# A row scale applied later, and VectorE's steps put into one fixed sequence, in a fused attention and SoLU kernel

## The chip, the core and the metric

The kernel runs on one core of one Trainium2 chip. A core has five engines that work side by side, each with a queue of its own that it goes through in order: TensorE (PE in the profile, its weight loads PEld), VectorE (DVE), ScalarE (ACT), GpSimd (POOL) and SyncE (SP, which issues transfers here). An instruction at the head of a queue waits for the semaphores of the work that it needs, and everything behind it on that engine waits too. The metric is the device time of one execution in microseconds (us), lower is better.

## What is computed

Two stages, 33280 tokens (8 x 4160) of width 192, all in float32.

```
# stage 1, 8 heads of 24 columns, 7 taps: a causal sliding sum with softmax weights
w   = softmax(weight_gen, axis=-1)             # (8, 4160, 8, 7); sum + 1e-9 below
x   = sum over k of w[..., k] * x_padded[s + k]
# stage 2
h    = x @ w_in                                # 192 -> 1024
e    = exp(h - max(h)); sm = e / (sum(e) + 1e-9)
solu = h * sm
ln   = (solu - mean) / sqrt(var + 1e-6) * g_ln # mean and var over the 1024
out  = ln @ w_out                              # 1024 -> 192
```

## The kernel before

The tokens are laid over 128 partitions as 128 runs of 260 tokens, and a **tile** t is the t-th token of every run: 260 tiles, each a 128 x 192 block of x and a 128 x 1024 block of h. Stage 1 works on groups of four tiles, its weights and x come in chunks of sixteen.

The steps have short names, and a table `ops` maps each to a function. For one group or chunk of stage 1:

- `t0` to `t6` (`softmax_taps`, lines 104 to 130): softmax of a chunk's weights, on DVE, POOL, ACT, DVE, ACT, DVE, POOL.
- `att` (`attention`, lines 132 to 152): three large GpSimd instructions for four tiles, the 7-tap product `pr` and two foldings that leave two or three partial sums in `half` (two buffers).
- `fin` (line 396): VectorE reduces `half` to `a` (three buffers of four tiles). `dup` (line 402): ScalarE copies columns.

For one tile, or a pair, of stage 2:

- `xT`, `xhi`, `xn`, `xlo` or `xld` (lines 407 to 448): transposes on PE, split of x into a high and a low part.
- `mm1` (line 459): ten matmuls of 512 columns into `h`, which has three PSUM buffers, so that `mm1` of tile t+3 waits for the last readers of tile t.
- `max` (line 473, DVE): minus the row maximum. `vb` (line 477, DVE): a bound, the larger of that maximum's size and 0.5. `vr` (line 482, DVE): its reciprocal, the row scale SIGMA.
- `exp` (line 486, ACT): the exponentials `e` and their sum. `solu` (line 492, DVE): h becomes h x SIGMA x e, in place, with the row sum. The profile shows the read of that sum as an instruction of its own, DVE_READ_ACCUMULATOR.
- `sq` (line 498, ACT): squares for the variance. `hi` (line 505, ACT): h x 2^14 rounded to float16. `lo` (line 509, DVE): the rest in float16. `sq` and `lo` read the same PSUM tile, and whichever comes later in the program waits for the other.
- `tr` (line 517, SP): a transposing transfer of both halves. `mm2` (line 561): 24 matmuls into `po`. `out` (line 572, ACT): the row's factor, and every four tiles a store.
- `f0` to `f7` (`scales`, lines 521 to 552): per group of four tiles, eight tiny instructions on [128, 4] statistics, alternately ACT and DVE, that make the row's factor.

**What sets the order.** The steps are not written in the order in which they run. `plan` (lines 651 to 793) lists every step with its engine, a duration and the steps that it follows, `issue_order` (lines 806 to 866) plays them against a model of the engines, and where several are ready takes the one with the lowest tile number plus a number of the table `URGENCY`. The order that comes out is the order of the engines' queues. On the chip nothing of the model is left but that order.

Of the kernel before, what the change touches and what calls it, by code (L numbers as in the profile page):

```python
# [9 lines left out]
F32 = mybir.dt.float32  # L10
# [10 lines left out]
MIDDLE, REACH = 1.01538, 0.061529  # L21

# [7 lines left out]
def tile_kernel(ctx: ExitStack, tc: tile.TileContext, x, weight_gen, w_in, w_out, g_ln, out):  # L30
    nc = tc.nc
# [277 lines left out]
    def prepare_second(step, half=None):  # L309
# [11 lines left out]
        elif step == 6:  # L321
# [9 lines left out]
            nc.vector.tensor_scalar_add(kinv, k, (127 - 73 + 1) << 23)  # L331
# [133 lines left out]
    ZE, SIGMA, Q, E, Y, V, Y2, R, OUT, M, Z, U, L, T, NMAX, HALF, BOUND = range(17)  # L465
    stats = const.tile([P, 6, TG, 17], F32, name="stats")
# [23 lines left out]
    def solu(t):  # L490
        h, e = h_of[t], e_of[t]
        nc.vector.scalar_tensor_tensor(  # L492
            out=h, in0=h, scalar=stat(t, SIGMA), in1=e, op0=ALU.mult, op1=ALU.mult, accum_out=stat(t, M)
        )
# [8 lines left out]
    def high_half(t):  # L503
        hl = hl_of[t] = big.tile([P, 2, FF], F16, name="hl", bufs=3)
        nc.scalar.activation(hl[:, 0, :], h_of[t], AF.Copy, scale=2.0**14)  # L505

    def low_half(t):
        hl = hl_of[t]
        nc.vector.scalar_tensor_tensor(  # L509
            out=hl[:, 1, :], in0=h_of[t], scalar=2.0**14, in1=hl[:, 0, :],  # L510
            op0=ALU.mult, op1=ALU.subtract,
        )
# [8 lines left out]
    def scales(t, step):  # L521
# [86 lines left out]
    for n in range(8):  # L608
        ops[f"f{n}"] = at(scales, n)
# [38 lines left out]
}  # L648


def plan(run, starts, group, stat_group, rows_left, on_vector, loads):
# [74 lines left out]
    for i, t in enumerate(groups):  # L726
# [13 lines left out]
    for t in range(0, run, 2):  # L740
        add("xT", t, PE, 355, 300, ("dup", group_of[t]), low_of(t - 2))
# [158 lines left out]
```

## Time and profile before

| | |
|---|---|
| median of three runs | 1310.42 us (1307.23 to 1311.84) |
| the profiled execution | 1309.91 us, of which the span from first to last instruction is 1308.1 |
| busy share of the span | PE 95%, DVE 95%, POOL 91%, ACT 88% |
| granted TensorE clock | 0.994 of full speed |
| `max`, `lo`, `solu` on DVE, 260 each | 1218, 1222 and 1283 ns |
| `exp`, `sq`, `hi` on ACT, 260 each | 1124, 1130 and 1027 ns |
| `vb`, `vr` on DVE, 260 each | 154 and 161 ns |

How to read it: a duration is that of one instruction from start to end, and two that follow each other on DVE or ACT overlap a little, so the distance from start to start is what an instruction costs its queue. Four engines are busy for nine tenths of the span, and no single line of the page says which of them holds the others up.

### The profile page before, as it was taken

The numbers are of one execution on the slowest core, as the hardware profiler recorded it, in microseconds if no ns is written. First come the engines' busy times: TensorE is split into PE (matmuls) and PEld (weight loads), VectorE is DVE, ScalarE is ACT, GpSimd is POOL, SyncE is SP. The second block draws the span as 40 slices with busy tenths as digits, with TensorE's granted clock in tenths as the row PEclk, the third lists the DMA queues.
The fourth block names the chain that finished last, engine by engine and source line by source line (L and its number), as shares of the span: only waits on it lengthen the run. The fifth ranks groups of instructions, "written<-read, shape, count | busy, mean of one in ns | idle before, by whom it ended". The sixth has DMA issues, their size and how long they took to land.

```text
span 1308.1 us, 25825 instructions
## 1 busy us (share of the span) xinstructions
PE 1239.4 (95%) x9574; PEld 1069.3 (82%) x9574; DVE 1247.9 (95%) x2055; ACT 1151.4 (88%) x2271; POOL 1195.8 (91%) x243
## 2 busy tenths in 40 slices
PE   1689999999999999999999999999999999999998
PEld 1577788788888888888888888888888888888887
DVE  6889999999999999999999999999999999999995
ACT  5778888899899989989898989989898998998896
POOL 6999989999999999999999999999999999999910
PEclk9899999999999999999999999999999999999999
DMA  8488658697787969777796987788797876975665
GB/s 236 87 184 181 144 130 175 136 203 140 165 174 144 212 127 204 140 174 167 151 205 132 199 143 167 170 162 189 137 203 141 176 165 141 199 140 119 132 139 130
DMA packets 565917, 211.35 MB, mean 162 GB/s; under 512 B 544552, under 2 KB 545960, under 8 KB 565792
## 3 DMA queue, kind: packets, MB, share of 16 engines
q1 hardware_dynamic: 565344, 208.14, 76.3%
q10 hardware_dynamic: 448, 1.57, 0.5%
q8 instruction: 75, 1.23, 0.4%
q14 instruction: 50, 0.41, 0.1%
HBM read 46.15 MB, written 25.56 MB: 55 GB/s over the span
## 4 chain that ended last, share of the span: by engine, by line
DVE 51%; ACT 24%; issue 16%; PE 7%; DMA 2%; ACTq 0%; SPq 0%; DVEq 0%
DVE h L492 19%; DVE stats L473 15%; ACT e L486 9%; DVE a L396 8%; ACT e L498 5%; ACT hl L505 5%; PE h L459 3%; PE po L561 3%; ACT x_hi L421 2%; DVE hl L509 2%; ACT ot L572 2%; DVE stats L477 2%; DVE wm L114 1%; DVE wm L122 1%; DVE stats L529 1%
## 5 line engine op out<-in xcount | busy, mean ns | idle before, releaser
L135 POOL TENSOR_TENSOR pr<-xt,wt 128x5376 f32<-128x5376 f32 (+1 forms) x66 | 631.4, 9567 | 10.2 <-DMA wt<-in_weight_gen_dram 7.5
L561 PE MATMUL po<-w_hl,hlT 128*128 128x192 f16 x6192 | 557.4, 247 | 13.6 <-ACT ot L572 11.7
L561 PEld LDWEIGHTS <-hlT 128*128 128x128 f16 x6240 | 513.9, 98 | 61.6 <-issue 55.4
L492 DVE SCALAR_TENSOR_TENSOR h<-h,stats,e 128x1024 f32<-128x1024 f32 x260 | 333.5, 1283 | 4.5 <-ACT e L486 4.4
L509 DVE SCALAR_TENSOR_TENSOR hl<-h,hl 128x1024 f16<-128x1024 f32 x260 | 317.7, 1222 | 6.6 <-ACT e L498 2.9
L473 DVE TENSOR_REDUCE stats<-h 128x1 f32<-128x1024 f32 x260 | 316.8, 1218 | 3.7 <-PE h L459 3.0
L486 ACT ACTIVATE e<-h,stats 128x1024 f32<-128x1024 f32 x260 | 292.2, 1124 | 19.1 <-DVE stats L473 10.4
L498 ACT ACTIVATE e<-h,stats 128x1024 f32<-128x1024 f32 x260 | 293.7, 1130 | 7.0 <-DVE hl L509 5.7
L505 ACT ACTIVATE hl<-h 128x1024 f16<-128x1024 f32 x260 | 266.7, 1027 | 25.3 <-DVE h L492 23.4
L459 PE MATMUL h<-wb,x_lo 128*128 128x512 f32 x784 | 216.2, 397 | 0.0
L459 PE MATMUL h<-wa_hi,x_hi 128*128 128x512 f32 x520 | 180.3, 428 | 18.1 <-ACT e L498 10.7
L459 PEld LDWEIGHTS h<-wb,x_lo 128*128 128x128 f32 x784 | 148.6, 190 | 35.7
L147 POOL TENSOR_TENSOR pr<-pr 128x2304 f32<-128x2304 f32 (+1 forms) x34 | 169.6, 4987 | 2.7
L142 POOL TENSOR_TENSOR half<-pr 128x2304 f32<-128x2304 f32 x32 | 164.1, 5128 | 2.5
L459 PE MATMUL h<-wa_hi,x_lo 128*128 128x512 f32 x520 | 164.9, 398 | 1.4 <-ACT x_lo L435 1.4
L459 PE MATMUL h<-wa_lo,x_hi 128*128 128x512 f32 x520 | 164.0, 396 | 0.8 <-DVE wa_lo L268 0.8
L396 DVE TENSOR_REDUCE a<-half 128x768 f32<-128x2304 f32 (+1 forms) x66 | 149.1, 2259 | 0.4
L572 ACT ACTIVATE ot<-po,stats 128x192 f32<-128x192 f32 x258 | 110.7, 429 | 9.5 <-PE po L561 7.6
L459 PEld LDWEIGHTS h<-wa_hi,x_lo 128*128 128x128 f32 x520 | 98.3, 189 | 24.9 <-ACT x_lo L435 1.8
L459 PEld LDWEIGHTS h<-wa_lo,x_hi 128*128 128x128 f32 x520 | 98.3, 189 | 23.7 <-DVE wa_lo L268 1.6
L149 POOL TENSOR_TENSOR half<-pr 128x1536 f32<-128x1536 f32 (+1 forms) x34 | 114.8, 3377 | 2.7
L413 PE MATMUL pa<-ident,a 128*128 128x128 f32 x520 | 80.4, 276 | 27.6 <-DVE a L396 25.2
(77 smaller groups left out, 1132.7 us busy)
## 6 DMA issues: line engine op xcount, KB each, us to landing
out_dram<-ot SPq DMA_DIRECT2D x65, 384.0 KB, 3.4
xt<-in_x_dram SPq DMA_DIRECT2D x30, 576.0 KB, 4.7
xt<-in_x_dram SPq DMA_DIRECT2D x30, 480.0 KB, 4.5
wt<-in_weight_gen_dram SPq DMA_DIRECT2D x15, 448.0 KB, 4.5
hlT<-hl SPq DMA_TRANSPOSE x260, 4.3
hlT<-in_moe_w_out_dram SPq DMA_DIRECT2D x4, 384.0 KB, 5.4
xt<-in_x_dram SPq DMA_DIRECT2D x3, 384.0 KB, 5.1
hlT<-in_moe_w_in_dram ACTq DMA_DIRECT2D x2, 512.0 KB, 9.2
```

What stands on the lines that cost most here:

```text
L135: nc.gpsimd.tensor_tensor(out=window(pr, 0, [(TG * D, K), (HG, n * H), (1, HG)]), in0=window(xt, t * D, [(D, K), (HG, n * H), (1, HG)]), i ...
L142: nc.gpsimd.tensor_tensor(out=half, in0=pr[:, :3], in1=pr[:, 3:6], op=ALU.add)
L147: nc.gpsimd.tensor_tensor(out=pr[:, :3], in0=pr[:, :3], in1=pr[:, 3:6], op=ALU.add)
L396: nc.vector.tensor_reduce(columns(t)[:, :, :D], half.rearrange("p j t d -> p t d j"), axis=AX.X, op=ALU.add)
L459: nc.tensor.matmul(h[:, fs], lhs, rhs[:, fs], start=n == 0, stop=n == len(terms) - 1)
L473: nc.vector.tensor_reduce(stat(t, NMAX), h_of[t], axis=AX.X, op=ALU.max, negate=True)
L486: nc.scalar.activation(e, h_of[t], AF.Exp, bias=stat(t, NMAX), accum_out=stat(t, Z))
L492: nc.vector.scalar_tensor_tensor(out=h, in0=h, scalar=stat(t, SIGMA), in1=e, op0=ALU.mult, op1=ALU.mult, accum_out=stat(t, M))
L498: nc.scalar.activation(e_of.pop(t), h_of[t], AF.Square, bias=stat(t, M), scale=-float(FF), accum_out=stat(t, Q),)
L505: nc.scalar.activation(hl[:, 0, :], h_of[t], AF.Copy, scale=2.0**14)
L509: nc.vector.scalar_tensor_tensor(out=hl[:, 1, :], in0=h_of[t], scalar=2.0**14, in1=hl[:, 0, :], op0=ALU.mult, op1=ALU.subtract,)
L561: nc.tensor.matmul(po[:, :D], hlT[:, half * NJ + j, :], w2_hl[:, j, w, :], start=n == 0, stop=n == len(terms) - 1,)
```

## The change

SIGMA no longer enters `solu`. There the factor is the constant `BOOST` = 2^10, and SIGMA becomes the scale operand of `hi` and of `lo`, one value per partition read from memory where a constant stood before. The statistics that follow are then those of the unscaled row, so that `f0` and `f1` (which multiplied the sum of exponentials by the bound) fall away, 67 of each in the run, `f2` takes the sum directly with a small bias tile `least`, and `f7` multiplies three values in place of two. The places in `stats` are renumbered for that.

In `plan`, a function `turn` ties VectorE's steps of a tile, from tile 4 on, to one sequence: `max` of t+1 behind `vr` of t, `lo` of t behind `max` of t+1, `vb` of t+1 behind `lo` of t, `solu` of t+1 behind `vb`, `vr` behind `solu`. `hi` now follows `vr`. Some of the model's durations change by a few ns, `fin` of three sums from 2480 to 2705 ns. `URGENCY` is unchanged. The order of all queues is worked out anew from this.

```diff
+BOOST = 2.0**10
...
-            nc.vector.tensor_scalar_add(kinv, k, (127 - 73 + 1) << 23)
+            nc.vector.tensor_scalar_add(kinv, k, (127 - 73 + 15) << 23)
...
+    EPSILON = 1e-3 * FF**1.5 * BOOST
+    least = const.tile([P, 1], F32, name="least")
+    nc.gpsimd.memset(least, EPSILON * 1e-9)
...
     def solu(t):
-            out=h, in0=h, scalar=stat(t, SIGMA), in1=e, op0=ALU.mult, op1=ALU.mult, accum_out=stat(t, M)
+            out=h, in0=h, scalar=BOOST, in1=e, op0=ALU.mult, op1=ALU.mult, accum_out=stat(t, M)
...
     def high_half(t):
-        nc.scalar.activation(hl[:, 0, :], h_of[t], AF.Copy, scale=2.0**14)
+        nc.scalar.activation(hl[:, 0, :], h_of[t], AF.Copy, scale=stat(t, SIGMA))
     def low_half(t):
-            out=hl[:, 1, :], in0=h_of[t], scalar=2.0**14, in1=hl[:, 0, :],
+            out=hl[:, 1, :], in0=h_of[t], scalar=stat(t, SIGMA), in1=hl[:, 0, :],
...
-        if step == 0:
-            nc.scalar.activation(of(ZE), of(Z), AF.Copy, bias=1e-9)
-        elif step == 1:
-            reduce(U, ZE, 2, ALU.mult)
-        elif step == 2:
-            nc.scalar.activation(of(E), of(U), AF.Square, scale=1e-3 * FF**1.5)
+        if step == 2:
+            nc.scalar.activation(of(E), of(Z), AF.Square, bias=least, scale=EPSILON)
...
-            reduce(OUT, Y2, 2, ALU.mult)
+            reduce(OUT, Y2, 3, ALU.mult)
...
+FIXED = 4
+    def turn(name, t):
+        return [(name, t, -9999)] if FIXED <= t < run else []
...
-        add("max", t, DVE, 1131, 84, ("mm1", t), ("exp", t - 4))
-        add("vb", t, DVE, 62, 84, ("max", t), ("f7", ...))
-        add("vr", t, DVE, 70, 93, ("vb", t))
+        add("max", t, DVE, 1131, 84, ("mm1", t), ("exp", t - 4), *turn("vr", t - 1))
+        add("vb", t, DVE, 62, 84, ("max", t), ("f7", ...), *turn("lo", t - 1))
+        add("vr", t, DVE, 80, 83, ("vb", t), *turn("solu", t))
-        add("solu", t, DVE, 1200, 89, ("exp", t), ("vr", t))
+        add("solu", t, DVE, 1200, 89, ("exp", t), *turn("vb", t))
-        add("hi", t, ACT, 904, 120, ("solu", t), ("tr", t - 3))
-        add("lo", t, DVE, 1131, 90, ("hi", t))
+        add("hi", t, ACT, 904, 120, ("solu", t), ("vr", t), ("tr", t - 3))
+        add("lo", t, DVE, 1131, 90, ("hi", t), *turn("max", t + 1))
```

Three places of the queues show what moved. In the rows the lines are those of each kernel's own text, where the changed one has `max` at 478, `vb` 482, `vr` 487, `exp` 491, `solu` 497, `sq` 503, `hi` 510, `lo` 514, `fin` 398; a number behind a name tells one buffer from another.

**VectorE, tile 132 of 260.** Before, from one `max` to the next:

```order
L473 TENSOR_REDUCE stats_137<-h_8115 128x1
L477 TENSOR_REDUCE stats_137<-stats_137 128x1
L529 TENSOR_REDUCE stats_137<-stats_137 128x4
L482 RECIPROCAL stats_137<-stats_137 128x1
L509 SCALAR_TENSOR_TENSOR hl_8168<-h_8049,hl_8168 128x1024
L492 SCALAR_TENSOR_TENSOR h_8115,stats_137<-h_8115,stats_137,e_8186 128x1024
L529 TENSOR_REDUCE stats_137<-stats_137 128x4
```

And the same tile now:

```order
L478 TENSOR_REDUCE stats_137<-h_8097 128x1
L534 TENSOR_REDUCE stats_137<-stats_137 128x4
L514 SCALAR_TENSOR_TENSOR hl_8145<-h_8009,stats_137,hl_8145 128x1024
L482 TENSOR_REDUCE stats_137<-stats_137 128x1
L497 SCALAR_TENSOR_TENSOR h_8097,stats_137<-h_8097,e_8159 128x1024
L534 TENSOR_REDUCE stats_137<-stats_137 128x4
L487 RECIPROCAL stats_137<-stats_137 128x1
```

`max`, `lo` of the tile before, `solu` stood in this sequence already; `vb` has moved behind `lo` and `vr` behind `solu`, so that neither follows directly on the instruction whose result it reads.

**ScalarE, tiles 206 to 208.** Before, between one `exp` and the next one:

```order
L486 ACTIVATE e_12638,stats_137<-h_12565,stats_137 128x1024
L572 ACTIVATE ot_12643<-po_12590,stats_137 128x192
L498 ACTIVATE e_12579,stats_137<-h_12500,stats_137 128x1024
L421 CAST x_hi_12675<-pa_12622 128x512
L505 ACTIVATE hl_12677<-h_12565 128x1024
L486 ACTIVATE e_12682,stats_137<-h_12627,stats_137 128x1024
```

And now, over two tiles:

```order
L491 ACTIVATE e_12622,stats_137<-h_12514,stats_137 128x1024
L573 ACTIVATE ot_12542<-po_12594,stats_137 128x192
L437 CAST x_lo_12644<-pa_12537 128x512
L510 ACTIVATE hl_12653<-h_12514,stats_137 128x1024
L503 ACTIVATE e_12622,stats_137<-h_12514,stats_137 128x1024
L491 ACTIVATE e_12686,stats_137<-h_12579,stats_137 128x1024
L537 ACTIVATE stats_137<-stats_137,least_138 128x4
L573 ACTIVATE ot_12542<-po_12661,stats_137 128x192
L510 ACTIVATE hl_12709<-h_12579,stats_137 128x1024
L503 ACTIVATE e_12686,stats_137<-h_12579,stats_137 128x1024
L423 CAST x_hi_12738<-pa_12656 128x512
L491 ACTIVATE e_12742,stats_137<-h_12633,stats_137 128x1024
```

Before, the `exp` of the next tile stood directly behind `hi`, and the `sq` of the tile before it ahead of `hi`. Now `sq` of the same tile, and in the second case a cast of x as well, stands between `hi` and the next `exp`.

**VectorE, where the last groups are reduced.** Before, the 51st of the 66 reductions `fin` (it makes tiles 196 to 199) and what stands around it:

```order
L473 TENSOR_REDUCE stats_137<-h_11665 128x1
L477 TENSOR_REDUCE stats_137<-stats_137 128x1
L482 RECIPROCAL stats_137<-stats_137 128x1
L509 SCALAR_TENSOR_TENSOR hl_11715<-h_11603,hl_11715 128x1024
L396 TENSOR_REDUCE a_11738<-half_11496 128x4x192
L529 TENSOR_REDUCE stats_137<-stats_137 128x4
```

And now:

```order
L514 SCALAR_TENSOR_TENSOR hl_11072<-h_10936,stats_137,hl_11072 128x1024
L482 TENSOR_REDUCE stats_137<-stats_137 128x1
L497 SCALAR_TENSOR_TENSOR h_10994,stats_137<-h_10994,e_11106 128x1024
L487 RECIPROCAL stats_137<-stats_137 128x1
L398 TENSOR_REDUCE a_11124<-half_10871 128x4x192
L478 TENSOR_REDUCE stats_137<-h_11047 128x1
```

Counted along the queue, 192 `max` stood ahead of this `fin` before (tiles 0 to 191), and 182 stand ahead of it now: the `max` in the last row is that of tile 182. Ahead of the last `fin` it was 251 and is 242. In tiles, `fin` ran four to six ahead of `max` from tile 40 on before; now the distance starts at five and grows to fifteen by tile 192, where it stays.

More of the change, by code (lines that the diff above doesn't have):

```diff
@@ L462, in first_product @@
         h_of[t] = h
-    ZE, SIGMA, Q, E, Y, V, Y2, R, OUT, M, Z, U, L, T, NMAX, HALF, BOUND = range(17)
-    stats = const.tile([P, 6, TG, 17], F32, name="stats")
+    Q, E, Y, V, Y2, R, BOUND, OUT, M, Z, L, T, NMAX, HALF, SIGMA = range(15)
+    stats = const.tile([P, 6, TG, 15], F32, name="stats")
+    EPSILON = 1e-3 * FF**1.5 * BOOST
+    least = const.tile([P, 1], F32, name="least")
+    nc.gpsimd.memset(least, EPSILON * 1e-9)
     nc.gpsimd.memset(stats[:, :, :, HALF], 0.5)
@@ L607, in tile_kernel @@
         ops[f"lx{n}"] = at_chunk(load_x, n)
-    for n in range(8):
+    for n in range(2, 8):
         ops[f"f{n}"] = at(scales, n)
@@ L731, in plan @@
             after += [(f"lx{k}", starts[c]) for k in range(loads)]
-        add("att", t, POOL, part * (16850 if three else 18480), 60, *after, ready=12000 if c == 1 else 7500)
+        add("att", t, POOL, part * (16850 if three else 18480), 60, *after, ready=14200)
         old = t // 4 * 4 - 12
-        add("fin", t, DVE, part * (2480 if three else 1697), 92, ("att", t), ("xT", old + 2 if old >= 0 else -1))
+        add("fin", t, DVE, part * (2705 if three else 1697), 92, ("att", t), ("xT", old + 2 if old >= 0 else -1))
         add("dup", t, ACT, 295 if group(t) == 4 else 200, 112, ("fin", t))
@@ L740, in plan @@
     for t in range(0, run, 2):
-        add("xT", t, PE, 355, 300, ("dup", group_of[t]), low_of(t - 2))
+        add("xT", t, PE, 362, 300, ("dup", group_of[t]), low_of(t - 2))
         add("xhi", t, ACT, 465, 115, ("xT", t), ("mm1", t - 3))
@@ L755, in plan @@
             after.append(("mm1", t - 1, -9999))
-        add("mm1", t, PE, 2328, 72, *after)
-        add("max", t, DVE, 1131, 84, ("mm1", t), ("exp", t - 4))
-        add("vb", t, DVE, 62, 84, ("max", t), ("f7", stats_of[t - 24] if t >= 24 else -1, -9999))
-        add("vr", t, DVE, 70, 93, ("vb", t))
+        add("mm1", t, PE, 2332, 72, *after)
+        add("max", t, DVE, 1131, 84, ("mm1", t), ("exp", t - 4), *turn("vr", t - 1))
+        add("vb", t, DVE, 62, 84, ("max", t), ("f7", stats_of[t - 24] if t >= 24 else -1, -9999), *turn("lo", t - 1))
+        add("vr", t, DVE, 80, 83, ("vb", t), *turn("solu", t))
         add("exp", t, ACT, 1089, 31, ("max", t), ("sq", t - 2, -9999))
-        add("solu", t, DVE, 1200, 89, ("exp", t), ("vr", t))
+        add("solu", t, DVE, 1200, 89, ("exp", t), *turn("vb", t))
         add("sq", t, ACT, 1089, 32, ("solu", t))
-        add("hi", t, ACT, 904, 120, ("solu", t), ("tr", t - 3))
-        add("lo", t, DVE, 1131, 90, ("hi", t))
+        add("hi", t, ACT, 904, 120, ("solu", t), ("vr", t), ("tr", t - 3))
+        add("lo", t, DVE, 1131, 90, ("hi", t), *turn("max", t + 1))
         add("tr", t, SP, 60, 0, ("lo", t), ("mm2", t - 6), dma=-2600)
@@ L767, in plan @@
         after += [("mm1", run - 1), ("out", t - 2)] if t >= run - 4 else [("out", t - 1)]
-        add("mm2", t, PE, 1923, 218, ("tr", t), *after)
+        add("mm2", t, PE, 1930, 218, ("tr", t), *after)
         add("out", t, ACT, 303, 125, ("mm2", t), ("f7", stats_of[t]), ("od", t // 4 * 4 - 5))
@@ L771, in plan @@
             tiles = range(t - n + 1, t + 1)
-            add("f0", t, ACT, 97, 116, *(("exp", u, -160) for u in tiles))
-            add("f1", t, DVE, 70, 87, ("f0", t), *(("vr", u) for u in tiles))
-            add("f2", t, ACT, 97, 116, ("f1", t))
+            add("f2", t, ACT, 97, 116, *(("exp", u, -160) for u in tiles))
             add("f3", t, DVE, 70, 87, ("f2", t), *(("sq", u) for u in tiles))
```

## The prediction

> **What bounds it now.** I read the page first, then a long steady stretch, then the queues of VectorE and ScalarE row by row, since the page alone leaves four engines equal.
>
> ```profile
> span 1308.1 us, 25825 instructions
> ...
> PE 1239.4 (95%) x9574; PEld 1069.3 (82%) x9574; DVE 1247.9 (95%) x2055; ACT 1151.4 (88%) x2271; POOL 1195.8 (91%) x243
> ...
> DVE 51%; ACT 24%; issue 16%; PE 7%; DMA 2%; ACTq 0%; SPq 0%; DVEq 0%
> ```
>
> The chain of waits runs over VectorE and ScalarE. The columns of the next two rows are the stretch, its length, and the busy time of PE, PEld, DVE, ACT and POOL; the two below them are pieces of the chain, the start of every second three-sum `fin`, eight tiles apart.
>
> ```profile
> 50.00:250.00 200.00, 179.64 (x1341) 154.85 (x1342) 184.98 (x297) 163.37 (x322) 191.34 (x42) 0.97 0.73 155
> 300.00:1150.00 850.00, 845.06 (x6600) 731.27 (x6599) 839.35 (x1383) 775.98 (x1524) 821.87 (x157) 1.00 0.81 166
> ```
> ```profile
> 288.52 2.80 DVE a L396
> ...
> 1122.13 2.81 DVE a L396
> ```
>
> Between them lie 22 steps of eight tiles: 833.6 / 176 = 4.74 us a tile. PE is busy 99.4% of the second stretch, VectorE 98.7%, GpSimd 96.7%, ScalarE 91.3%. So nothing can go much below 4.71 us a tile whatever VectorE saves: PE's own work is 0.994 x 4.74. That is the first thing against a large gain. VectorE's queue over one plain tile, `solu` to `solu`:
>
> ```profile
> 632.96 1.28 DVE L492 SCALAR_TENSOR_TENSOR h<-h,stats,e 128x1024 f32<-128x1024 f32 x1
> 634.15 0.14 DVE L492 DVE_READ_ACCUMULATOR h<-h,stats,e 128x1 f32 x1
> 634.15 1.22 DVE L473 TENSOR_REDUCE stats<-h 128x1 f32<-128x1024 f32 x1
> 635.41 0.15 DVE L477 TENSOR_REDUCE stats<-stats 128x1 f32<-128x2 f32 x1
> 635.60 0.16 DVE L482 RECIPROCAL stats<-stats 128x1 f32<-128x1 f32 x1
> 635.68 1.22 DVE L509 SCALAR_TENSOR_TENSOR hl<-h,hl 128x1024 f16<-128x1024 f32 x1
> 636.82 1.28 DVE L492 SCALAR_TENSOR_TENSOR h<-h,stats,e 128x1024 f32<-128x1024 f32 x1
> ...
> 638.02 1.22 DVE L473 TENSOR_REDUCE stats<-h 128x1 f32<-128x1024 f32 x1
> ```
>
> Start to start, 634.15 to 638.02: `max` 1.26, `vb` 0.19, `vr` 0.08, `lo` 1.14, `solu` 1.20, together 3.87 us.
>
> **The VectorE part.** `vb` reads what `max` writes, and `vr` what `vb` writes. Where an independent reduction follows `max`, it starts sooner:
>
> ```profile
> 656.40 1.21 DVE L473 TENSOR_REDUCE stats<-h 128x1 f32<-128x1024 f32 x1
> 657.53 1.07 DVE L114 TENSOR_REDUCE wm<-wt 128x128 f32<-128x896 f32 x1
> ```
>
> 1.13 in place of 1.26. With other work between, `max` costs 1.13, `vb` about 0.08 (as `vr` to `lo`), `lo` 1.14, `solu` 1.20, `vr` 0.08: 3.63, a saving of 0.24 us a tile, some 60 us of VectorE time for the run. The Trainium skill, VectorE: DVE Perf Modes, section "Rules for kernel authors", says of chained operations that the pipeline drains after each one regardless, so that only their number counts. By that rule the regrouping saves nothing and only `f1` does; the two rows differ by 0.13 us and speak against it, so I keep the saving, and the rule is a rival below.
>
> The saving is not the whole loop, though. `solu` of the next tile needs its `exp`, `exp` needs `max`, and `lo` needs `hi`. The rows for ScalarE:
>
> ```profile
> 634.33 1.02 ACT L505 ACTIVATE hl<-h 128x1024 f16<-128x1024 f32 x1 [0.43 <-DVE h L492]
> ...
> 636.51 0.57 ACT L421 CAST x_hi<-pa 128x512 fp32r<-128x512 f32 x1
> 636.98 1.13 ACT L498 ACTIVATE e<-h,stats 128x1024 f32<-128x1024 f32 x1
> ...
> 638.08 0.43 ACT L572 ACTIVATE ot<-po,stats 128x192 f32<-128x192 f32 x1
> ...
> 639.33 1.12 ACT L486 ACTIVATE e<-h,stats 128x1024 f32<-128x1024 f32 x1
> ```
> ```profile
> 1210.66 1.13 ACT L486 ACTIVATE e<-h,stats 128x1024 f32<-128x1024 f32 x1
> ```
> ```profile
> 1211.91 1.29 DVE L492 SCALAR_TENSOR_TENSOR h<-h,stats,e 128x1024 f32<-128x1024 f32 x1 [0.36 <-ACT e L486]
> ```
>
> `max` at 638.02 to its `exp` at 639.33: 1.31. `exp` at 1210.66 to a `solu` that waits for it: 1.25. With `max` 1.20 + 0.08 behind `solu`, the loop `solu`, `vr`, `max`, `exp`, `solu` takes 1.28 + 1.31 + 1.25 = 3.84 us, against 3.87 before. So on a plain tile the new order gains 0.03 us, 6 us in 200 tiles; the rest becomes a wait for `exp`. Where a weight reduction or `xld` stands between `max` and `lo`, VectorE is the longer path, and about 0.12 of the saving stays: some 37 such tiles, 4 us. `f1` goes: 67 pieces of 0.08, 5 us. Credit: 15 us.
>
> **The scale operand.** `hi` now reads its scale from memory. This operation in this form is not in the trace; the neighbours are (the second number behind the bar is the mean in ns):
>
> ```profile
> L505 ACT ACTIVATE hl<-h 128x1024 f16<-128x1024 f32 x260 | 266.7, 1027 | 25.3 <-DVE h L492 23.4 <-DVE stats L529 0.4
> L572 ACT ACTIVATE ot<-po,stats 128x192 f32<-128x192 f32 x258 | 110.7, 429 | 9.5 <-PE po L561 7.6 <-PE pa L413 1.2 <-issue 0.6
> L421 ACT CAST x_hi<-pa 128x512 fp32r<-128x512 f32 x130 | 76.6, 589 | 4.2 <-PE pa L413 2.1 <-PE h L459 1.8
> ...
> L342 ACT ACTIVATE w_hl<-h,k 128x768 f16<-128x768 f32 x2 | 1.8, 892 | 0.0
> ```
>
> Constants first: 1027 at 1024 columns and 589 at 512 make 0.855 ns a column and 151 ns fixed. By that line L342 and L572, whose scale comes from memory, would take 808 and 315, and take 892 and 429. So +84 to +114; L342 is the same operation, and I take 0.09 us for `hi`. Ends: 0 and 0.11. `lo` gains the operand and `solu` loses it: nothing, between -0.06 and +0.06 each, as their 1222 and 1283 differ.
>
> ```profile
> 612.67 1.00 ACT L505 ACTIVATE hl<-h 128x1024 f16<-128x1024 f32 x1
> 613.57 1.11 ACT L498 ACTIVATE e<-h,stats 128x1024 f32<-128x1024 f32 x1
> ```
>
> `hi` thus holds ScalarE's queue 0.90 + 0.09 = 0.99. It starts when `vr` is done, 1.20 + 0.16 behind `solu`, and 0.04 for the signal (as from the read's end at 634.29 to `hi` at 634.33): 1.40 (before 634.33 - 632.96 = 1.37): hidden under `max` on plain tiles. The dropped `f0` returns ScalarE 0.1 us per four tiles, off the path. `least`, one small memset at the start, and `f7` over three values cost nothing: the gaps that `f7` waits in are ScalarE's.
>
> **The order on ScalarE, the largest term.** The queue now often has `sq` between `hi` and the next `exp`. Counted over tiles 40 to 239, with no `fin`, `xld` or softmax step on VectorE to fill the time: 23 times `sq` alone, 25 times `sq` with a cast of x; before, never. Behind `solu`: `hi` starts at 1.40, `sq` at 2.39, and takes 1.10 of queue (636.98 to 638.08), `exp` at 3.49, the next `solu` at 4.74. But `lo` now also comes behind `sq`, which shares its tile:
>
> ```profile
> 1272.12 0.21 ACT L498 ACTIVATION_READ_ACCUMULATOR e<-h,stats 128x1 f32 x1
> ```
> ```profile
> 1272.36 1.23 DVE L509 SCALAR_TENSOR_TENSOR hl<-h,hl 128x1024 f16<-128x1024 f32 x1 [0.47 <-ACT e L498]
> ```
>
> 0.24 from that read to `lo`: 2.39 + 1.00 + 0.24 = 3.63, plus `lo` 1.14 and `vb` 0.08 is 4.85. With the cast (0.47 of queue, 636.51 to 636.98), `exp` starts at 3.96 and `solu` at 5.21. Excess over 3.84: 23 x 1.01 + 25 x 1.37 = 57 us. Without `hi`'s 0.09 it would be 53. Tiles 240 on are PE's (the tail has no `fin`), and up to tile 40 I assume the old pace.
>
> **Sum.** 1308 + 57 - 15 = 1350 for the span, 4.95 us a tile over the 200 tiles; the profiled execution's own time stands 1.8 above its span and 0.5 under the median of the runs: 1352. Uncertain are the waits of VectorE (0 to 57, some fall where PE is late anyway) and the credit (0 to 60).
>
> **A floor from GpSimd.** The new order puts the 51st `fin` ahead of `max` of tile 182, where 192 `max` stood ahead of it before. GpSimd's instructions are unchanged, so that `fin` can't come much earlier:
>
> ```profile
> POOL wt L128 <- DVE stats L482: 16.0, 9, 2.8
> ...
> POOL wt L128 <- DVE wy L126: 6.8, 2, 5.1
> ```
> ```profile
> 967.76 1.82 POOL L143 TENSOR_TENSOR half<-half,pr 128x768 f32<-128x768 f32 x1
> ```
> ```profile
> 971.06 2.80 DVE L396 TENSOR_REDUCE a<-half 128x768 f32<-128x2304 f32 x1
> ```
> ```profile
> 925.27 1.22 DVE L473 TENSOR_REDUCE stats<-h 128x1 f32<-128x1024 f32 x1
> ```
>
> Its data were done at 969.6. GpSimd had waited 16.0 + 6.8 us for weights behind its first product; with none of that, 946.8, and 2.8 for `fin`: `max` 182 at 949.6 or later. Before, it ran at 925.27 (the 183rd of its kind) and 382.8 us were left. At PE's 4.71 instead of 4.74 these become 380: 1330, or 1325 if PE is one tile further ahead than before. So the run can be hardly faster than 1327 on the clock, even if ScalarE never delays anything.
>
> **Rivals.**
> - *Floor alone* (1327 to 1337): the `sq` in front of `exp` falls where `max` waits for PE anyway, and only GpSimd's lead counts. For it: PE at 99.4%. Against: 48 places. 0.18.
> - *Faster* (1285 to 1305): between 50 and 250 us PE stands idle for 20.4 us of 200; a freer VectorE fills that, and 200 steady tiles run at 4.71 (-6): 1284 at best. It decides only if GpSimd delivers the 51st group 25 us or more below its floor, that is, if its products run shorter than now because VectorE disturbs them less. Nothing in the trace speaks for that. 0.06.
> - *No change* (1307 to 1314): PE's 4.74 holds, and the moved `fin` waits for nothing. The floor speaks against it. 0.05.
> - *No saving* (1366 to 1380): consecutive dependent reductions cost the same wherever they stand, the skill's rule above. Then the credit is `f1` alone, or less, and the waits remain: 1308 + 57 + 1.8 = 1367 and more. 0.09.
> - Mine (1337 to 1366): 0.62.
>
> Faster or slower by 0.3%, 4 us, is what a measurement of this kernel can tell. Slower 0.89, same 0.05, faster 0.06. The range 1327 to 1369 leaves out the two low cases and the upper part of the fourth.
>
> **What would show it.** Two waits of VectorE (us in total, times, longest) and GpSimd's last row, before:
>
> ```profile
> DVE h L492 <- ACT e L486: 4.4, 8, 1.4
> ...
> DVE hl L509 <- ACT e L498: 2.9, 6, 0.7
> ```
> ```profile
> 1242.62 3.48 POOL L149 TENSOR_TENSOR half<-pr 128x1536 f32<-128x1536 f32 x1
> ```
>
> In the changed profile `max` should fall to about 1.13 of queue, `hi` rise to about 1115 ns; VectorE's share fall below 93% with waits of `solu` for `exp` and of `lo` for `sq` of 20 us or more each, where the waits before have 4.4 and 2.9; PE's share fall to 92%; and the time from GpSimd's last row to the end of the span grow from 62 us (1308.1 less 1242.62 + 3.48) to 90 or more. I am wrong if VectorE stays at 95% with few such waits, or GpSimd's instructions are shorter.

## The result and the profile after

The changed kernel takes 1398.2 us, median of four runs (1395.66 to 1400.96), against 1308.83 for the kernel before on the same chip (1306.39 to 1311.84): 1.0682 times as long, 95% interval 1.0648 to 1.0716. That is slower by 89 us where 43 were forecast, and outside the range. The profiled execution took 1400.96 us. The page's first rows:

```profile
span 1398.9 us, 25456 instructions
...
PE 1263.7 (90%) x9574; PEld 1078.0 (77%) x9574; DVE 1218.9 (87%) x1988; ACT 1186.3 (85%) x2204; POOL 1195.6 (85%) x244
```

VectorE works 29 us less than before (1247.9) and the span is 91 us longer: its idle time grew from 60 to 180 us. The stretches shown for before, again with the busy time of PE, PEld, DVE, ACT and POOL, then the granted clock and the transfers:

```profile
50.00:250.00 200.00, 173.51 (x1204) 145.64 (x1205) 166.55 (x267) 155.64 (x290) 189.66 (x40) 0.91 0.69 145
300.00:1150.00 850.00, 798.35 (x6137) 681.72 (x6137) 769.32 (x1241) 743.90 (x1377) 818.88 (x157) 1.00 0.76 157
```

In the long stretch PE fell from 845 to 798 us, VectorE from 839 to 769, ScalarE from 776 to 744. GpSimd alone kept its share, 819 us where it had 822, and is now the busiest. When the other three fall together, none of them is the bound, and the waits between them have to be read. The granted clock is 1.00 in this stretch before and now, so it is not what slows it; in the first stretch it is 0.91 where it was 0.97, and no run separates its part there. The groups of the large operations (busy time and mean ns of one, then the idle time ahead of them and what ended it):

```profile
L514 DVE SCALAR_TENSOR_TENSOR hl<-h,stats,hl 128x1024 f16<-128x1024 f32 x260 | 333.5, 1283 | 77.6 <-ACT e L503 44.4 <-ACT hl L510 31.2
L497 DVE SCALAR_TENSOR_TENSOR h<-h,e 128x1024 f32<-128x1024 f32 x260 | 318.7, 1226 | 10.1 <-ACT e L491 7.7
...
L510 ACT ACTIVATE hl<-h,stats 128x1024 f16<-128x1024 f32 x260 | 289.0, 1112 | 53.0 <-DVE stats L487 49.7 <-DVE h L497 0.8
...
L573 ACT ACTIVATE ot<-po,stats 128x192 f32<-128x192 f32 x258 | 108.4, 420 | 45.0 <-PE po L562 38.7 <-DVE stats L534 2.5 <-issue 1.4
```

And the waits (us in total, times, longest):

```profile
ACT hl L510 <- DVE stats L487: 49.7, 72, 2.2
DVE stats L534 <- ACT e L503: 46.9, 43, 2.3
DVE hl L514 <- ACT e L503: 44.4, 41, 2.3
...
ACT ot L573 <- PE po L562: 38.7, 62, 2.0
DVE hl L514 <- ACT hl L510: 31.2, 93, 1.9
...
DVE h L497 <- ACT e L491: 7.7, 35, 1.0
```

Before, `lo` for `sq` (L503 here) had 2.9 us, and the other two waits of VectorE had:

```profile
DVE stats L529 <- ACT e L498: 4.3, 4, 2.1
...
DVE hl L509 <- ACT hl L505: 2.5, 5, 1.2
```

Two stretches of ScalarE's and VectorE's queues show how they arise:

```profile
1105.08 1.13 ACT L491 ACTIVATE e<-h,stats 128x1024 f32<-128x1024 f32 x1
...
1107.46 0.42 ACT L573 ACTIVATE ot<-po,stats 128x192 f32<-128x192 f32 x1 [0.83 <-PE po L562]
1107.84 1.11 ACT L510 ACTIVATE hl<-h,stats 128x1024 f16<-128x1024 f32 x1
1108.85 1.11 ACT L503 ACTIVATE e<-h,stats 128x1024 f32<-128x1024 f32 x1
...
1109.94 0.58 ACT L423 CAST x_hi<-pa 128x512 fp32r<-128x512 f32 x1
1110.40 1.14 ACT L491 ACTIVATE e<-h,stats 128x1024 f32<-128x1024 f32 x1
```
```profile
1106.49 1.22 DVE L497 SCALAR_TENSOR_TENSOR h<-h,e 128x1024 f32<-128x1024 f32 x1
...
1107.71 1.21 DVE L478 TENSOR_REDUCE stats<-h 128x1 f32<-128x1024 f32 x1
1110.08 0.17 DVE L534 TENSOR_REDUCE stats<-stats 128x4 f32<-128x8 f32 x1 [1.17 <-ACT e L503]
1110.16 1.28 DVE L514 SCALAR_TENSOR_TENSOR hl<-h,stats,hl 128x1024 f16<-128x1024 f32 x1
...
1111.66 1.23 DVE L497 SCALAR_TENSOR_TENSOR h<-h,e 128x1024 f32<-128x1024 f32 x1 [0.16 <-ACT e L491]
```

ScalarE stands 0.83 us at `out`, which waits for PE; `hi` and `sq` queue behind it. On VectorE the tiny `f3` (L534) is next after `max`, it needs that `sq`, and `lo` stands behind `f3`. `lo` would hardly have started sooner without `f3`: in the program it comes behind the same `sq`, which reads the same PSUM tile. So 1.17 us pass with nothing done. This `solu` starts at 1106.49 and the next one at 1111.66, 5.17 us later.

Where along the run the time went is read from the starts of `max` of tile 40 and tile 240, before and then now:

```profile
254.96 1.24 DVE L473 TENSOR_REDUCE stats<-h 128x1 f32<-128x1024 f32 x1
...
1200.53 1.22 DVE L473 TENSOR_REDUCE stats<-h 128x1 f32<-128x1024 f32 x1
```

```profile
272.56 1.21 DVE L478 TENSOR_REDUCE stats<-h 128x1 f32<-128x1024 f32 x1
...
1289.25 1.21 DVE L478 TENSOR_REDUCE stats<-h 128x1 f32<-128x1024 f32 x1
```

The start is 17.6 us longer (15 of them by tile 20), the 200 tiles 71.1 (5.08 us a tile where 4.73 stood), the rest 2. These three numbers carry the comparison of all runs; each row is from the profiled execution except for the medians and ratios.

| kernel | median us | ratio to before (95%) | `max` of tile 40 at | us a tile, 40 to 240 |
|---|---|---|---|---|
| before | 1308.4 to 1309.9 | 1 | 255.0 | 4.73 |
| changed | 1398.2 | 1.0682 (1.0648 to 1.0716) | 272.6 | 5.08 |
| 1 new arithmetic, old order | 1314.4 | 1.0037 (1.0024 to 1.0050) | 255.6 | 4.75 |
| 2 the same, `vb`, `vr` moved | 1323.2 | 1.0110 (1.0093 to 1.0127) | 264.8 | 4.74 |
| 3 changed, constant in `hi` | 1383.6 | 1.0565 (1.0548 to 1.0581) | 266.7 | 5.02 |
| 4 old order from tile 40 on | 1329.7 | 1.0155 (1.0137 to 1.0172) | 270.7 | 4.76 |
| 5 changed, `sq` behind `exp` | 1512.3 | 1.1549 (1.1528 to 1.1569) | 283.5 | 5.52 |
| 6 changed, `sq` behind both | 1427.9 | 1.0894 (1.0865 to 1.0924) | 271.6 | 5.19 |
| 7 changed, `sq` behind `lo` | 1500.8 | 1.1464 (1.1447 to 1.1481) | 277.8 | 5.54 |
| 8 changed, `f3` later | 1450.2 | 1.1071 (1.1053 to 1.1090) | 277.2 | 5.29 |
| 9 old order, new places of `sq` | 1495.0 | 1.1414 (1.1382 to 1.1446) | 255.0 | 5.58 |
| 10 old order, new `mm2`, `out` | 1545.0 | 1.1795 (1.1777 to 1.1813) | 260.6 | 5.79 |
| 11 old order, new stage 1 | 1472.6 | 1.1243 (1.1226 to 1.1259) | 266.5 | 5.48 |
| 12 as 9, with `f2` to `f7` | 1560.0 | 1.1902 (1.1866 to 1.1938) | 259.7 | 5.87 |
| 13 before, one number of the plan | 1339.0 | 1.0225 (1.0210 to 1.0239) | 248.8 | 4.91 |
| 14 changed, no fixed sequence | 1351.8 | 1.0317 (1.0303 to 1.0331) | 256.2 | 4.89 |
| 15 changed, one number of the plan | 1342.4 | 1.0266 (1.0249 to 1.0283) | 254.5 | 4.89 |
| 16 changed, table fitted anew | 1302.0 | 0.9945 (0.9934 to 0.9957) | 247.2 | 4.72 |
| 17 as 16, no fixed sequence | 1307.1 | 0.9982 (0.9973 to 0.9990) | 256.8 | 4.71 |

### The profile page after: what moved, and what is told of

Same layout as the page of the kernel before. It is cut to its first block, busy times and chain, and to the rows that moved or that the text cites. A ratio compares the mean times of both kernels' runs of the same rounds, so it can differ in the third digit from the quotient of the medians.

```text
span 1398.9 us, 25456 instructions
## 1 busy us (share of the span) xinstructions
PE 1263.7 (90%) x9574; PEld 1078.0 (77%) x9574; DVE 1218.9 (87%) x1988; ACT 1186.3 (85%) x2204; POOL 1195.6 (85%) x244
## 5 line engine op out<-in xcount | busy, mean ns | idle before, releaser
L514 DVE SCALAR_TENSOR_TENSOR hl<-h,stats,hl 128x1024 f16<-128x1024 f32 x260 | 333.5, 1283 | 77.6 <-ACT e L503 44.4
L510 ACT ACTIVATE hl<-h,stats 128x1024 f16<-128x1024 f32 x260 | 289.0, 1112 | 53.0 <-DVE stats L487 49.7
L497 DVE SCALAR_TENSOR_TENSOR h<-h,e 128x1024 f32<-128x1024 f32 x260 | 318.7, 1226 | 10.1 <-ACT e L491 7.7
L503 ACT ACTIVATE e<-h,stats 128x1024 f32<-128x1024 f32 x260 | 289.7, 1115 | 11.0 <-DVE h L497 5.6
L573 ACT ACTIVATE ot<-po,stats 128x192 f32<-128x192 f32 x258 | 108.4, 420 | 45.0 <-PE po L562 38.7
L461 PEld LDWEIGHTS h<-wa_hi,x_hi 128*128 128x128 f32 x520 | 79.5, 191 | 55.5 <-DVE stats L482 17.2
```

The costliest lines, as they stand in the source:

```text
L461: nc.tensor.matmul(h[:, fs], lhs, rhs[:, fs], start=n == 0, stop=n == len(terms) - 1)
L497: nc.vector.scalar_tensor_tensor(out=h, in0=h, scalar=BOOST, in1=e, op0=ALU.mult, op1=ALU.mult, accum_out=stat(t, M))
L503: nc.scalar.activation(e_of.pop(t), h_of[t], AF.Square, bias=stat(t, M), scale=-float(FF), accum_out=stat(t, Q),)
L510: nc.scalar.activation(hl[:, 0, :], h_of[t], AF.Copy, scale=stat(t, SIGMA))
L514: nc.vector.scalar_tensor_tensor(out=hl[:, 1, :], in0=h_of[t], scalar=stat(t, SIGMA), in1=hl[:, 0, :], op0=ALU.mult, op1=ALU.subtract,)
```

## The experiments

The theory after reading both profiles: the loss is in the new order of the queues, `sq` in front above all. Rivals: the memory scale of `hi`; the wait of `hi` for `vr`; the fixed sequence on VectorE as such.

### Arithmetic apart from order (runs 1 and 2)

Run 1 makes the order with the plan of before and leaves `f0` and `f1` out of it:

```diff
-    for op, t in issue_order(plan(RUN, ...)):
+    for op, t in keep_order([x for x in issue_order(plan_before(RUN, ...)) if x[0] not in ("f0", "f1")], ...):
```

`keep_order` goes through a given order and puts a step later only where a link asks for it.

> The arithmetic of the changed kernel (scale in hi and lo, f0 and f1 gone) in the order of the kernel before. If the order is to blame (ScalarE's sq ahead of exp, lo and f3), nothing of the 89 us is left: 1305 to 1312 us, with hi at about 1112 ns. If the memory scale of hi is to blame (0.085 us x 260), up to 1330. If hi's new wait for vr is to blame, waits of hi for VectorE's line of vr appear; none are expected, since vr stands ahead of solu here.

1314.4 us: 5 us slower than before, by an interval that leaves out 1, and 2 us over the first band. The page's groups show `hi` with the memory scale and without a wait for `vr`:

```profile
L510 ACT ACTIVATE hl<-h,stats 128x1024 f16<-128x1024 f32 x260 | 290.6, 1119 | 27.9 <-DVE h L497 27.2
```

`hi` costs 92 ns more than before (1027), 24 us of ScalarE's time in the run; the whole new arithmetic makes the run 5 us longer. So about 84 of the 89 us belong to the order.

Run 2 adds the VectorE part alone to that order:

```diff
+    more = [x for t in range(4, RUN) for x in ((("lo", t - 1), ("vb", t)), (("solu", t), ("vr", t)))]
```

> As the run before it, but in VectorE's queue vb stands directly behind lo of the tile before and vr directly behind solu; all else keeps the order of before. If the regrouping is harmless by itself: 1300 to 1312 us, max at 1.13 us of queue, VectorE's share some 4 points lower. If the regrouping itself does the harm, because hi now starts behind vr and solu no longer covers it: over 1330, with ScalarE's waits for vr of 40 us or more.

1323.2 us. VectorE's work falls by 30 us (from 1247.0 in run 1; the first row is run 2's), and its idle time grows from 66 to 104:

```profile
PE 1243.6 (94%) x9574; PEld 1070.5 (81%) x9574; DVE 1217.2 (92%) x1988; ACT 1170.9 (89%) x2204; POOL 1195.8 (91%) x244
```
```profile
POOL wt L130 <- DVE wy L128: 39.2, 14, 7.6
DVE hl L514 <- ACT hl L510: 35.7, 98, 1.3
...
ACT hl L510 <- DVE stats L487: 34.8, 50, 1.7
```

From tile 40 to 240 it needs 948.4 us against 949.5 in run 1: the regrouping neither gains nor loses there, where PE is busy for 842 of the 850 us of the long stretch. The 9 us lie between tiles 20 and 40, in the start. Neither end of the expectation came; the harm of more than 1330 did not, and the gain did not either.

### The scale operand in the new order (run 3)

```diff
-        nc.scalar.activation(hl[:, 0, :], h_of[t], AF.Copy, scale=stat(t, SIGMA))
+        nc.scalar.activation(hl[:, 0, :], h_of[t], AF.Copy, scale=2.0**4)
```

> The changed kernel with a constant in hi where the row's scale stood, so that the output is scaled wrongly; hi is then short again (1027 ns) and does not wait for vr. If the memory scale and its wait are a large part: 1340 to 1375. If they are hidden or small: 1375 to 1395, since hi stands in ScalarE's queue ahead of the sq that VectorE waits for, 48 times about 0.1 us for the operand and 72 times up to 0.2 for the wait.

The row's scale is left out of `hi` here. 1383.6 us, 15 less than the changed kernel, in the second of the two bands. `hi` is back at 1021 ns. Measured over those `hi` that waited, it starts a median 1.316 us behind the start of `solu` here and 1.341 in the changed kernel: the wait for `vr` is worth 25 ns a tile. The operand, with that wait, is a real cost and a sixth of the loss in this order, where in run 1 the whole arithmetic costs 5.

### Where along the run (run 4)

```diff
+    cut = order[: order.index(("lo", 39))]
+    order = cut + [x for x in old if x not in set(cut)]
```

> The arithmetic of the changed kernel; its order up to lo of tile 39, and from there on all that is left in the order of the kernel before. By the traces, the start is worth 17 us and the steady part 71: 1325 to 1340 if the regions add up. If a poor start costs later too (GpSimd behind): 1340 to 1360. If the steady part does not depend on the order: over 1380.

1329.7 us. The start of the new order costs 15 us against run 1 (270.7 against 255.6 at tile 40), and from there the old order runs at its old pace, 4.76. The regions add up, and the order from tile 40 on is worth 68.5 us (1398.2 less 1329.7). The plan of the change also moves the earliest start of GpSimd's products, `ready` of `att`, from 7500 or 12000 to 14200 ns, which the text of the change does not name; no run tells its part in the start apart.

### One place at a time, taken back (runs 5 to 8)

```diff
+    more = [(("exp", t + 1), ("sq", t)) for t in range(4, RUN - 1)]     # run 5
+    more = run 5's + [(("lo", t), ("sq", t)) for t in range(4, RUN - 1)]     # run 6
+    more = [(("lo", t), ("sq", t)) for t in range(4, RUN - 1)]     # run 7
+    more = [(("solu", t + 1), ("f3", t)) for t in range(7, RUN - 1, 4)]     # run 8
```

> The changed kernel with one thing added to its order: sq of each tile from 4 on comes behind exp of the next tile (where f3 stood in between it comes later too). If sq ahead of exp, lo and f3 is what holds VectorE up, the waits of lo for sq (44 us) and of the small reductions for sq (47 us) mostly go and the time falls by 50 to 75 us: 1325 to 1350. If sq's place does not matter, 1385 to 1405.

1512.3 us where 1325 to 1350 was expected: the theory in this form falls. In 59 tiles `sq` still stood ahead of `lo`, and now behind an `exp` as well. Both waits that the edit aims at (44.4 and 46.9 us) grow:

```profile
DVE hl L514 <- ACT e L503: 114.1, 49, 3.7
...
DVE stats L534 <- ACT e L503: 85.8, 50, 3.0
```

> The changed kernel with sq of each tile behind both exp of the next tile and lo of its own, as in the kernel before; in the run with exp alone, 59 sq stayed ahead of lo and lo waited for them 114 us. If sq's place is the cause of the 89 us: 1315 to 1345, waits of lo for sq under 10 us and of f3 under 15. If the order of the rest is to blame (the casts of x, out, fin, the start): over 1370 with other waits in their place.

1427.9 us. No `sq` is left ahead of `exp` or `lo`, `lo` no longer waits for it, and the kernel is still 30 us slower than the changed one. The wait has moved to `f3`, and to the `mm1` that needs the PSUM tile which `sq` reads:

```profile
DVE stats L534 <- ACT e L503: 72.3, 52, 2.6
PEld h L461 <- ACT e L503: 61.5, 75, 3.1
```

> The changed kernel with sq behind lo of its own tile, and no more: exp of the next tile still comes behind it. If it is lo's wait for sq that costs (44 us), 1350 to 1365. If it is exp's wait behind sq, that wait grows by what sq now waits for lo: 1390 to 1430, with solu waiting for exp 30 us or more.

1500.8 us, above even the second band: `solu` waits 106.7 us for its `exp`, behind a `sq` that waits 96.5 for `lo`.

> The changed kernel with f3 moved behind solu of the tile that follows its group, away from its place between max and lo, where VectorE stood 46.9 us waiting for sq. If that wait is on the path: 1350 to 1375. If lo behind it would have waited as long for the same sq: 1385 to 1400, with the 47 us found at lo instead.

1450.2 us. `lo` waits 52 us more for `sq` than it did (44.4), as the second theory said; but the time, which should then have stayed, rose by 52 as well:

```profile
DVE hl L514 <- ACT e L503: 96.8, 84, 3.4
ACT stats L541 <- DVE stats L534: 69.6, 53, 2.9
```

The second row is new: `f4` (L541) now stands at the head of ScalarE's queue and waits for the later `f3`. Run 5 lengthens the waits that it aims at, runs 6 to 8 take theirs away and find them again elsewhere, and all four lose. A step that is put later in these queues makes what was ordered around it wait.

### One place at a time, brought into the old order (runs 9 to 12)

On the base of run 1 (1314.4 us), from tile 40 on, the named steps are put behind the same neighbour as in the new order, and what they need is pulled ahead of them:

```diff
+    order = set_like(old, new, links, [(("sq",), ("exp", "hi"))], 40)     # 9, with sq or lo first as in new
+    ... [(("mm2",), ("mm1",)), (("out",), ("exp", "hi"))]     # 10
+    ... [(("fin", "t0", "t3", "t5"), ("max", "lo", "solu")), (("dup", "t2", "t4"), ("exp", "hi"))]     # 11
+    ... run 9's + [(("f3", "f5", "f7"), ("max", "lo", "solu")), (("f2", "f4", "f6"), ("exp", "hi"))]     # 12
```

> The arithmetic of the changed kernel in the order of before (1314 us), with one thing taken over from the new order, from tile 40 on: the place of sq against exp and hi on ScalarE, and whether sq or lo of a tile comes first. If sq's place is what costs 70 us in the steady part: 1350 to 1385. If it costs only together with the rest: 1318 to 1335. If the prediction's own term was right in size: 57 us, 1371.

1495.0 us, over all three numbers and 181 over run 1. `sq` stands ahead of the next `exp` with no fill in 67 tiles here, in 56 in the changed kernel, in 3 in run 1. Of these tiles 58 lie between 40 and 239; from `solu` to `solu` they take 5.32 us on the mean, 1.4 more than the 3.93 of run 1's plain tiles, which is what the prediction had for such a place (1.0 to 1.4). That makes 81 of the 168 us that the 200 tiles lose. The waits of run 9 say where more was lost:

```profile
POOL wt L130 <- DVE stats L487: 168.4, 11, 19.3
PE po L562 <- ACT ot L573: 112.9, 71, 5.2
DVE hl L514 <- ACT e L503: 69.5, 69, 2.5
...
DVE h L497 <- ACT e L491: 40.4, 27, 3.4
```

The waits of VectorE that were priced are there. But GpSimd's softmax steps get their input from VectorE's queue, and wait 168 us when that queue is late (the row names `vr`, which stands beside the softmax step in the queue); in the old order GpSimd was 96.7% busy and four tiles ahead.

> The same base, with the place of mm2 among mm1 and of out on ScalarE taken over from the new order from tile 40 on: both come one tile earlier there, out of a tile behind exp of the 4th or 5th tile after it where it stood behind the 5th or 6th. If this shorter lead makes ScalarE wait for PE with hi and sq queued behind: 1340 to 1385, with waits of out for PE of 30 us or more. If not: 1314 to 1322.

1545.0 us, far over the first band. `out` for PE has 181.8 us in 97 waits, `lo` for `hi` behind it 84.1. Coming one tile earlier, `mm2` and `out` cost more here than any other single family. The edit is not clean, though: `out` needs `f7`, so some 90 steps `f3`, `f5` and `f7` come to other places on VectorE too, so its 231 us are not those of `mm2` and `out` alone.

> The same base, with the places of fin, dup and the softmax steps taken over from the new order from tile 40 on, so that the lead of fin grows to 14 tiles. The prediction's floor from GpSimd says at least 1327; 1327 to 1340 if GpSimd then sets the end, with VectorE waiting for GpSimd. If the lead costs nothing: 1312 to 1320. A share in the 70 us beyond the floor would need over 1350.

1472.6 us: over 1350, so the lead costs beyond the floor, but by more than the 70 us that it was to have a share in. VectorE does wait for GpSimd, but the larger rows are of others:

```profile
POOL wt L118 <- DVE stats L482: 83.9, 8, 20.3
ACT a L404 <- DVE a L398: 70.2, 40, 9.9
...
DVE a L398 <- POOL half L145: 25.1, 3, 10.2
```

> As the run with sq's place, and the places of f2 to f7 taken over as well, so that f3 stands between max and lo and waits for sq there. If f3's wait for sq (46.9 us in the changed kernel) is a cause of its own: 20 to 45 us above the run with sq alone. If lo waits for the same sq anyway: within 6 us of it.

1560.0 us, 65 above run 9. The `f` steps are a cause of their own there, larger than expected.

So each piece of the new order, put with what it needs into the old one, costs 158 to 231 us over run 1, while all pieces together cost 84. The loss is not a sum over families of steps, and no single one can be called its cause.

### The table and the sequence (runs 13 to 17)

What remained was what made the order. Run 13 is the kernel before, arithmetic and all, with one of the change's numbers in the plan:

```diff
-        add("fin", t, DVE, part * (2480 if three else 1697), 92, ...)
+        add("fin", t, DVE, part * (2705 if three else 1697), 92, ...)
```

> The kernel before with one number of its plan changed, fin of three sums 2480 to 2705 ns as in the change, and the order made anew with the same table; arithmetic as before. If a table that no longer fits the plan is enough to lose time: 1325 to 1350. If the order takes such a number without harm: 1305 to 1315.

1339.0 us. No instruction differs, only the order that the same `URGENCY` yields, and 2.25% are lost (interval 2.10 to 2.39).

> The changed kernel without the fixed sequence on VectorE (turn off for all tiles), all other numbers and the table as they are. If the sequence is the whole harm: 1310 to 1320. If the table is a cause by itself: 1330 to 1360. If the sequence is harmless: 1385 or more.

1351.8 us with `FIXED = 260`, in the second band: half of the loss stays without the fixed sequence, so the old table with the changed plan costs by itself. The sequence under this table costs the other half.

```diff
-        add("hi", t, ACT, 904, 120, ("solu", t), ("vr", t), ("tr", t - 3))
+        add("hi", t, ACT, 995, 120, ("solu", t), ("vr", t), ("tr", t - 3))
```

> The changed kernel with one number of its plan changed: hi at 995 ns in place of 904, the 0.09 us that the memory scale costs; sequence and table as they are. Its order has sq ahead of exp with nothing to fill the time 4 times, where the changed kernel has 56. If sq ahead of exp goes with the loss, whatever else stands in the order: 1330 to 1350. If it takes a new table: 1380 or more.

1342.4 us, run 15, 56 less than the changed kernel, with sequence and table untouched. That is in the band of `sq` ahead of `exp`, and the number is truer (`hi` grew by 85 ns on the chip). Neither is shown to be the reason: one number changed the whole order in run 13 too, run 15 with 4 such places is still 28 us slower than run 1 with 3, and run 17 below has 15 and loses nothing.

Runs 16 and 17 keep that number and have `URGENCY` and `PATIENCE` searched anew, with the sequence and without: entries altered at random, and kept where the plan's own model of the engines ends earlier with them. Run 16 differs from run 15 in these tables alone.

> The changed kernel with its fixed sequence, but hi at 995 ns in the plan and the tables URGENCY and PATIENCE searched anew for it. In its order sq never stands ahead of exp of the next tile, mm2 comes one or two tiles later than in the changed kernel, out likewise, and fin stays four tiles ahead. If the sequence by itself is harmless and the order made the 89 us: 1298 to 1314. If the sequence costs by itself (hi behind vr, VectorE in lockstep): 1325 or more.

> As the run before it, but without the fixed sequence, the tables searched anew for that. If the sequence neither gains nor costs: within 6 us of the run before it. If VectorE's shorter queue is worth something that only the fixed sequence brings, it is slower by 10 us or more; if the sequence costs, faster by as much.

1302.0 and 1307.1 us. Both are in the bands that call the sequence harmless (5 us apart, though their intervals don't touch). Run 16 is 40 us faster than run 15 by its tables alone. It is the change, sequence and all, and it beats the kernel before by 0.55% (0.43 to 0.66). Its busy times, its waits, and its steady stretch:

```profile
PE 1234.7 (95%) x9574; PEld 1055.1 (81%) x9574; DVE 1214.6 (93%) x1988; ACT 1171.8 (90%) x2204; POOL 1197.0 (92%) x244
```
```profile
DVE hl L514 <- ACT hl L510: 18.4, 57, 1.4
...
DVE hl L514 <- ACT e L503: 14.6, 19, 2.3
...
DVE stats L534 <- ACT e L503: 6.4, 2, 4.1
```
```profile
300.00:1150.00 850.00, 846.04 (x6614) 724.29 (x6613) 825.42 (x1344) 794.61 (x1490) 834.37 (x160) 1.00 0.82 167
```

PE is full again, 99.5%. VectorE has 33 us less to do than before and the 200 steady tiles take 944.7 us against 945.6: the saving buys nothing there. The 7.5 us come from the start (`max` of tile 40 at 247.2, before 255.0). Whether they are owed to VectorE's freed time or to the new search is open: a table searched anew for the kernel before was not run, and run 13, with the old arithmetic, also reaches tile 40 earlier (248.8). What is shown is that the sequence is harmless in an order that was made for it.

Two things that can be read off these orders go with the loss. The first is the lead of `fin` over `max`. It grows from four to 13, 12 and 13 tiles in runs 13, 14 and 15 (to 15 in the changed kernel), and stays at four to six in the kernel before and in runs 16 and 17. GpSimd is then the busiest engine of the long stretch; run 13:

```profile
300.00:1150.00 850.00, 820.56 (x6380) 706.39 (x6380) 821.71 (x1335) 755.33 (x1478) 828.97 (x158) 1.00 0.77 161
```

Its last row ends at 1235.6 us there, 10 earlier than before, but 90 us of the run follow the start of the last `fin`, where it was 59. So a growing lead can cost time behind an engine whose work is fixed, as the prediction's floor has it. Only run 11 changes the lead by itself, in an order not made for it, so its share of the loss is not shown.

The second is the model itself. Played with each kernel's own plan and table, `issue_order` ends (the largest value in `ended`) at 1272.5 us for the kernel before and at 1346.8 for the changed one; at 1303.5, 1305.9 and 1311.9 for runs 13 to 15, at 1278.2 and 1276.0 for runs 16 and 17. Over the kernel before that is 74, 31, 33, 39, 6 and 4 us, where the chip shows 89, 30, 42, 34, -7 and -2. So the plan's own model says that the old table is a poor one for the changed plan, and nearly by how much.

## The prediction, point by point

**The direction and VectorE's prices: right; the amount saved and the credit: not.** `max` followed by independent work takes 1.12 to 1.13 us of queue now, and `hi` 1112 ns where 1115 was forecast. `lo` and `solu` exchanged the cost of their operand (1222 to 1283, 1283 to 1226). VectorE's work fell by 29 us, where some 60 were forecast: the 0.24 us of a plain tile were applied to all 260, and in only 123 of them did `vr` stand directly behind `vb` before, and 13 us of it had been idle time ahead of `vb` and `vr`, not work. The credit of 15 us did not come: run 2, which has the regrouping alone, is 9 us slower than run 1. PE's 4.71 us a tile held; runs 16 and 17 reach 4.72 and 4.71. The drain rule of the Trainium skill, VectorE: DVE Perf Modes, section "Rules for kernel authors", was a rival; the distance from `max` to the next instruction is a median 1.25 us in run 1, where `vb` follows and reads it, and 1.12 before an independent `f3` in the changed kernel, so here the trace differs from it.

**The scale operand: right in size, its cover only half right.** Forecast 0.09 us hidden on plain tiles; 0.085 to 0.092 measured; 15 us in the new order (with the wait for `vr`), and in the old one no more than the 5 us of the whole arithmetic.

**The order on ScalarE: its 48 places right, "the rest at the old pace" the step that failed.** The term was sized as 48 places times an excess of 1.01 or 1.37 us. From one `solu` to the next, over tiles 40 to 239, sorted by what stands in the order:

| changed kernel | tiles | mean us | forecast |
|---|---|---|---|
| `sq` ahead of `exp`, nothing to fill the time | 23 | 4.89 | 4.85 |
| the same, with a cast of x | 25 | 5.23 | 5.21 |
| `exp` first, nothing to fill | 65 | 4.02 | 3.84 |
| `fin`, `xld` or a softmax step in between | 87 | 5.91 | none |

The 48 places take 243 us where 242 were forecast, 56 more than at the 3.90 that such tiles without a fill took before. The chain is right too: in the stretch shown, one of the 25, `hi`, `sq`, `exp` and the next `solu` start 1.35, 2.36, 3.91 and 5.17 us behind `solu`, and 1.40, 2.39, 3.96 and 5.21 were forecast. Only the wait shows up at another row. `lo` for `sq` came (44.4 us), `solu` for `exp` did not (7.7, forecast 20 or more), since `f3`, which needs the same `sq` and stands ahead in the queue, takes it first (46.9). The quoted rows of the new order show `f3` between `max` and `lo`, and the prediction leaves it out.

What failed is the assumption that nothing but these places costs. The other 152 tiles were to keep the old pace less the credit, and took 16 us more than before (with 48 tiles at 3.90 taken off the total of before). VectorE stands idle for 38 us in them, where it was 12.5 in all 200 tiles before, and 22 of the 38 are `lo` waiting for a late `hi`. The prediction has no such wait. `hi` queues behind `out`, which waits 38.7 us for PE in the run, as in the stretch shown, and `mm2` and `out` come a tile earlier in the new order; how much of the 22 us this makes is not measured. Runs 9 to 12 show that a wait does not end where it arises but is handed on to the queue behind, up to GpSimd, and runs 5 to 8 that the places can't be taken back one at a time.

**"Up to tile 40 the old pace", priced at nothing: wrong.** The start costs 17.6 us, and run 4 has 15 of them with the rest of the order as before.

**The sum.** Forecast for the span 1350, measured 1398.9. Of the missing 49, 29 lie in the 200 tiles (71 against 57 less 15), practically all of them outside the 48 places; 17.6 lie in the start, 2 in the tail.

**The floor.** The time from GpSimd's last row to the end grew as forecast (90 or more):

```profile
1262.73 3.50 POOL L151 TENSOR_TENSOR half<-pr 128x1536 f32<-128x1536 f32 x1
```

1398.9 less 1266.2 is 133 us. But VectorE was not held there: its list of waits has no row for `fin` waiting for GpSimd, which itself waited 57 us. The 51st `fin` started at 991.4 us, 12 behind its data, and `max` of tile 182 at 994.1, where the floor allows 949.6. The longer lead is there all the same, and runs 13 to 15 give it weight: 100 us of the run follow the start of the last `fin` here, 59 before.

**The rivals.** "No saving" ended nearest in time (1366 to 1380). Its reason, the drain rule, isn't so here, though the saving indeed brought no time. None of the rivals, and no chance, was put on the order as a whole being poor, though the change's text says that `URGENCY` is unchanged while the plan is not. Run 13 prices that doubt, 29.5 us for one number, and the plan's own model, played for the changed kernel, ends 74 us later than for the one before.

## What to carry to other kernels

Where an order is made by a plan and a table of priorities, a change to the plan is to be judged with a table searched for it: the change cost 89 us with the old table and won 7 with a new one (and one truer duration), while one altered number in the unchanged kernel lost 30. How the old table was made is not known here. Before such a change is run, the plan's own model can be played with it; here it showed the loss.

Where four engines are all some 90% busy, counting places and pricing each by its chain gave the right cost of those places and 56 of the 89 us. The rest was in tiles that looked unchanged and in the start. So look at what is queued behind each small waiting step (`f3`, `out`), and at an engine with fixed work whose results are asked for earlier. Relieving VectorE gained nothing in the steady part, where the profile has PE at 99%.

## What the runs showed of the hardware that was not expected

A row scale read from memory in place of a constant costs a 1024-column operation of ScalarE 85 to 92 ns (1027 to 1112 and 1119), and one of VectorE with three operands some 60 (`solu` 1283 to 1226 without it, `lo` 1222 to 1283 with it). Both sizes had been forecast from rows of neighbours, and both held. On VectorE a reduction followed by the instruction that reads its result holds the queue longer here than one followed by other work: `max` a median 1.25 us against 1.12 to 1.13, `vb` 0.19 against 0.06. An instruction of ScalarE that waited for `vr` began a median 0.04 us behind its end, as forecast.
